# Issuing the keys' sign rows from ScalarE instead of the sync engine

## The chip, the cores and the metric

The kernel runs on one core of one Trainium2 chip. The metric is device microseconds of one execution, lower is better. Engines are named as in the profile: PE (TensorE), DVE (VectorE), ACT (ScalarE), POOL (GpSimd), SP (the sync engine, which here does nothing but issue transfers).

## The reference

Three layers run one after the other on 2 batches of 768 tokens, in float32.

```python
# 1: attention of 8 heads of 64, masked by a hash of 6 sign bits
q_bits = (einsum('bhsd,dk->bhsk', q, proj) > 0); k_bits = (einsum('bhsd,dk->bhsk', k, proj) > 0)
mask = bucket(q_bits)[:, :, :, None] == bucket(k_bits)[:, :, None, :]
scores = where(mask, scale * q @ k.T, -1e9); attn_out = softmax(scores) @ v
# 2: token mixing of low rank (U, V), then a feed-forward layer 512 -> 2048 -> 512 with a residual
u = x + (x.T @ U @ V).T;  x = u + relu(u @ w_ch1) @ w_ch2
# 3: four attention experts with a causal mask, two of them chosen per token by a gate
out += gate[e] * (softmax(causal(scale * q_e @ k_e.T)) @ v_e) @ wo[e]
```

Only the first layer is touched: a query sees a key only where all six sign bits agree.

## The kernel before

Every large product is made of float16 halves (a high part and a rest), so that it keeps float32's precision. The first layer goes through 8 pairs of heads (2 batches, 4 pairs each). For one pair the operands are AQ, AK (the high parts and rests), BQ, BK (64 rows of products' rests, and below them 32 rows of signs, rows 64 to 95, `SIGN`). `a1_head` makes the scores of 128 queries against 768 keys by a matmul of AQ and AK (L621) and one of BQ and BK over 96 rows (L626); the sign rows add a large number where the bits differ, which is the mask. DVE takes the row's extreme (L632), ACT the exponential (L543), ACT and POOL split the result into halves HL (L545, L551), a transposing transfer turns HL into PT (L643), and PE multiplies PT with V (L555 to L557). Some tiles are transposed on PE instead (L597).

The operands of the next pair are prepared while the present pair's heads run: `a1_prep` (L443 on) loads and splits q and k and moves rows into place with twelve transfers (L452 to L463), and six head tiles later `signs` (L466 on) multiplies the operands with the projection (L477), turns the result into sign rows in one DVE instruction (L482, tile SG), and moves those rows in four transfers of 32 rows x 768 float16: for each of the two heads one into BQ (L486) and one into BK (L487). This happens for pairs 1 to 7, so 28 transfers; pair 0 writes its signs in place. The same stage, up to about 300 us, loads and splits the weights of layer two (L277, L280) and begins its matmuls (L748, L770).

All transfers of the program are issued from SP's queue. The order of the instructions within every engine, SP among them, is laid down when the program is built: a planner takes instructions by a priority that follows the program text and by when its own timeline has them ready. An engine runs its list strictly in that order. Each transfer raises one of eight completion semaphores; the program uses the eight in turn, in the planned order of the transfers, and a transfer is issued only once the transfer that had the semaphore before it, the eighth before, has landed.

Of the kernel before, what the change touches and what calls it, by code (L numbers as in the profile page):

```python
# [22 lines left out]
def kernel(  # L23
# [17 lines left out]
    nc = tc.nc  # L41
# [86 lines left out]
    def halves(n):  # L128
        return [(c, min(512, n - c)) for c in range(0, n, 512)]
# [240 lines left out]
    def later(n, fn):  # L370
        pending.append([n, fn])
# [39 lines left out]
    SIGN = slice(D, D + 32)  # L411
# [3 lines left out]
    def a1_operands(b, p):  # L415
        n = f"{b}_{p}"
        AQ = sp.tile([P, 2, S], FH, tag="AQ", bufs=2, name=f"AQ_{n}")
        AK = sp.tile([P, 2, S], FH, tag="AK", bufs=2, name=f"AK_{n}")
        V = sp.tile([P, 2, 2 * NT, D], FH, tag="V", bufs=2, name=f"V_{n}")
        BQ, BK = BQK[p % 2]  # L420
        preps[b, p] = (AQ, AK, BQ, BK, V)
        return preps[b, p]
# [20 lines left out]
    def a1_prep(b, p, wait):  # L443
        qn, kn, vn = nats.pop((b, p))
        n = f"{b}_{p}"
        AQ, AK, BQ, BK, V = a1_operands(b, p)
        TQ = sp.tile([P, 2, S], FH, tag="TQ", name=f"TQ_{n}")
        HQ, LQ = TQ[:, 0], TQ[:, 1]
        nc.scalar.activation(HQ, qn, AF.Copy, scale=-0.125)
        nc.vector.scalar_tensor_tensor(LQ, HQ, 8.0, qn, op0=ALU.mult, op1=ALU.add)  # L450
        for j, o in enumerate(HALF):
            nc.sync.dma_start(AQ[HALF[0], j], HQ[o])  # L452
            nc.sync.dma_start(AQ[HALF[1], j], LQ[o])
            nc.sync.dma_start(BQ[HALF[0], j], HQ[o])
        TK = sp.tile([P, 3, S], FH, tag="TK", name=f"TK_{n}")
        HK, SK, LK = TK[:, 0], TK[:, 1], TK[:, 2]
        nc.scalar.activation(HK, kn, AF.Copy)
        SKE(SK, kn, HK)
        KLE.tensor_tensor(LK, kn, HK, op=ALU.subtract)
        for j, o in enumerate(HALF):  # L460
            nc.sync.dma_start(AK[HALF[0], j], HK[o])
            nc.sync.dma_start(AK[HALF[1], j], SK[o])
            nc.sync.dma_start(BK[HALF[0], j], LK[o])  # L463
        a1_values(b, p, vn, V)

        def signs():  # L466
            sg = psc.tile([P, 1024], F32, tag="sc", name=f"sg_{n}")
            for c0, cn in halves(S):
                cs = slice(c0, c0 + cn)

                for last, ops in enumerate((
                    [(PQ, AQ[:, j]) for j in range(2)] + [(PK, AK[:, j]) for j in range(2)],
                    [(PL, AQ[:, j]) for j in range(2)]
                    + [(PB, BK[HALF[0], j]) for j in range(2)],
                )):
                    for i, (w, x) in enumerate(ops):
                        nc.tensor.matmul(  # L477
                            sg[32 * i : 32 * (i + 1), cs], w, x[:, cs],
                            start=(last == 0), stop=(last == 1), skip_group_check=True,
                        )  # L480
            SG = sp.tile([P, S], FH, tag="KS", bufs=2, name=f"SG_{n}")
            nc.vector.tensor_scalar(  # L482
                SG, sg[:, 0:S], thr[:, 0:1], far, op0=ALU.is_lt, op1=ALU.mult
            )
            for j in range(2):
                nc.sync.dma_start(BQ[SIGN, j], SG[32 * j : 32 * (j + 1)])  # L486
                nc.sync.dma_start(BK[SIGN, j], SG[64 + 32 * j : 96 + 32 * j])  # L487

        later(wait, signs)

    def a1_values(b, p, vn, V):
        f32 = any(x[0] == "F" for x in A1_MODES[b][p])
        V32 = VF[p % 2] if f32 else vn
        nc.gpsimd.tensor_scalar(V32, vn, 16.0, 1.0, op0=ALU.mult, op1=ALU.mult)
        nc.scalar.activation(V[:, 0], V32, AF.Copy)
        nc.gpsimd.tensor_tensor(V[:, 1], V32, V[:, 0], op=ALU.subtract)
# [814 lines left out]
```

## Time and profile before

| | us |
|---|---|
| median of three runs | 607.75 |
| the three runs | 604.22, 607.75, 609.76 |
| the profiled execution | 604.46 |
| its span, first to last instruction | 602.7 |

The time is device time of one execution. The profile is of one execution; its span is counted from the first to the last instruction of the program, and 604.46 - 602.7 = 1.8 us lie around it. Instruction durations are read from this execution. "SPq" marks an issue on SP's queue: its duration is the time that the issuing takes, not the transfer's way to its destination; the time from issue to landing is shown apart.

### The profile page before, as it was taken

Reading aid. Unit: us, or ns where it says so; the run is one execution under the profiler, and the core shown is the slowest. Engines: PE = TensorE matmul, PEld = TensorE weight load, DVE = VectorE, ACT = ScalarE, POOL = GpSimd, SP = SyncE. Lnnn points to the kernel's source line nnn. Section 1 sums busy time; section 2 is a strip of 40 time slices with the busy share of each in tenths; the row PEclk is TensorE's granted clock in tenths of the full one; section 3 lists DMA queues with packets and bytes.
Section 4 is the critical chain, followed back from the end, with each engine's and each line's share of the span. In section 5 each row is a group of like instructions: output and inputs, shape, how many; then the busy total and the mean of one; then the engine's idle time right before and its main releaser. Section 6 shows DMA issues by size and latency. Waiting matters only on the chain.

```text
span 602.7 us, 14989 instructions
## 1 busy us (share of the span) xinstructions
PE 555.8 (92%) x5982; PEld 416.1 (69%) x5982; DVE 412.1 (68%) x948; ACT 351.9 (58%) x753; POOL 260.3 (43%) x239
## 2 busy tenths in 40 slices
PE   3789996899899999799999989999999998999995
PEld 1468864776555545447888866878877898999754
DVE  6976897759999999858768455553564335455584
ACT  6798787767564665645768534672465216144683
POOL 6644579745967698622246400250134002002350
PEclk9889999999899999999999999999999999999998
DMA  8789899989999999782479910153046002004655
GB/s 268 170 174 179 225 209 263 187 216 216 316 190 208 237 216 240 159 197 63 92 133 141 177 25 10 36 94 92 4 86 125 36 1 46 12 18 41 121 106 114
DMA packets 176566, 82.00 MB, mean 136 GB/s; under 512 B 160368, under 2 KB 167152, under 8 KB 176496
## 3 DMA queue, kind: packets, MB, share of 16 engines
q1 hardware_dynamic: 176496, 81.04, 62.2%
q8 instruction: 47, 0.77, 0.6%
q14 instruction: 23, 0.19, 0.1%
HBM read 29.30 MB, written 3.15 MB: 54 GB/s over the span
## 4 chain that ended last, share of the span: by engine, by line
PE 59%; DVE 16%; DMA 11%; issue 5%; ACT 5%; POOL 2%; SPq 1%; DVEq 0%; ACTq 0%; POOLq 0%
PE px L824 12%; PE ph L806 11%; DMA PT<-HL 6%; PE px L770 3%; PE po L606 3%; DVE P L632 2%; PE pk L875 2%; PE pq L875 2%; PE sc L621 2%; PE sc L626 2%; PE pv L903 2%; PE ph L748 2%; PE pz L1106 2%; PE s L974 2%; DMA wx<-in_moe_w_ch_dram 2%
## 5 line engine op out<-in xcount | busy, mean ns | idle before, releaser
L551 POOL TENSOR_TENSOR HL<-P,HL 128x768 f16<-128x768 f32 (+5 forms) x91 | 121.3, 1338 | 258.4 <-ACT HL L545 197.2
L543 ACT ACTIVATE P<-P,m 128x768 f32<-128x768 f32 (+5 forms) x110 | 89.4, 813 | 40.7 <-DVE P L632 26.2
L806 PE MATMUL ph<-U,W 128*128 128x256 f16 (+1 forms) x960 | 95.4, 251 | 0.5 <-DVE hT L808 0.5
L824 PE MATMUL px<-hT,W 128*128 128x256 f16 (+1 forms) x960 | 94.1, 251 | 0.0
L824 PEld LDWEIGHTS <-W 128*128 128x128 f16 x960 | 78.2, 98 | 8.4
L806 PEld LDWEIGHTS <-W 128*128 128x128 f16 x960 | 77.0, 98 | 8.7 <-issue 0.8
L632 DVE TENSOR_SCALAR_CACHE_REDUCE P<-sc 128x768 f32<-128x768 f32 x80 | 74.9, 947 | 11.0 <-PE sc L626 10.9
L545 ACT ACTIVATE HL<-P 128x768 f16<-128x768 f32 (+5 forms) x91 | 63.1, 696 | 9.7 <-DMA PT<-HL 8.5
L555 PEld LDWEIGHTS <-PT 128*128 128x128 f16 x522 | 47.6, 98 | 16.8 <-DMA PT<-HL 8.3
L621 PE MATMUL sc<-AK,AQ 128*128 128x512 f16 x192 | 49.0, 335 | 6.2 <-DVE P L632 2.7
L556 PEld LDWEIGHTS <-PT 128*128 128x128 f16 x522 | 47.4, 98 | 5.4 <-issue 1.9
L555 PE MATMUL po<-V,PT 128*128 128x64 f16 x378 | 43.5, 193 | 6.6 <-DMA PT<-HL 3.2
L626 PE MATMUL sc<-BK,BQ 96*128 96x512 f16 x192 | 49.6, 336 | 0.0
L557 PEld LDWEIGHTS <-PT 128*128 128x128 f16 x522 | 47.5, 98 | 1.7 <-issue 0.2
L770 PE MATMUL px<-hT,W 128*128 128x512 f16 x192 | 44.4, 379 | 0.8 <-DVE acc L754 0.4
L808 DVE SCALAR_TENSOR_TENSOR hT<-ph,hT 128x256 f16<-128x256 f32 (+1 forms) x80 | 28.8, 366 | 23.1 <-ACT hT L807 22.3
L557 PE MATMUL po<-V,PT 128*128 128x64 f16 x378 | 44.2, 193 | 0.0
L556 PE MATMUL po<-V,PT 128*128 128x64 f16 x378 | 44.2, 193 | 0.0
L807 ACT ACTIVATE hT<-ph 128x256 f16<-128x256 f32 (+1 forms) x80 | 26.4, 334 | 28.9 <-PE ph L806 28.0
L748 PE MATMUL ph<-U,W 128*128 128x512 f16 x156 | 36.3, 380 | 1.7 <-DVE hT L756 1.3
L982 DVE TENSOR_SCALAR_CACHE_REDUCE P<-s 128x128 f32<-128x128 f32 (+5 forms) x48 | 29.3, 620 | 9.1 <-PE s L979 8.0
L770 PEld LDWEIGHTS <-W 128*128 128x128 f16 x192 | 18.1, 98 | 20.6 <-DVE acc L754 0.8
(257 smaller groups left out, 1252.1 us busy)
## 6 DMA issues: line engine op xcount, KB each, us to landing
w<-in_moe_w_ch_dram SPq DMA_DIRECT2D x17, 512.0 KB, 5.1
wx<-in_moe_w_ch_dram SPq DMA_DIRECT2D x15, 512.0 KB, 5.6
vn<-in_v_dram SPq DMA_DIRECT2D x8, 384.0 KB, 4.5
out_dram<-o SPq DMA_DIRECT2D x12, 256.0 KB, 2.1
kn<-in_k_dram SPq DMA_DIRECT2D x7, 384.0 KB, 4.6
qn<-in_q_dram SPq DMA_DIRECT2D x7, 384.0 KB, 4.0
AK<-TK SPq DMA_DIRECT2D x28, 96.0 KB, 2.7
AQ<-TQ SPq DMA_DIRECT2D x28, 96.0 KB, 3.1
```

Source lines behind the costliest of these rows:

```text
L543: nc.scalar.activation(P32, P32, AF.Exp, bias=m, scale=-1.0, accum_out=ssum)
L545: nc.scalar.activation(HL[:, 0], P32, AF.Copy)
L551: eng.tensor_tensor(HL[:, 1], P32, HL[:, 0], op=ALU.subtract)
L555: nc.tensor.matmul(o, PT[:, t, :], vh(t), start=(t == 0), stop=False)
L556: nc.tensor.matmul(o, PT[:, t, :], vl(t), start=False, stop=False)
L557: nc.tensor.matmul(o, PT[:, nk + t, :], vh(t), start=False, stop=(t == nk - 1))
L621: nc.tensor.matmul(ps[:, c0 : c0 + cn], aq[:, P * t : P * (t + 1)], ak[:, c0 : c0 + cn], start=True, stop=False,)
L626: nc.tensor.matmul(ps[:, c0 : c0 + cn], bq[:, P * t : P * (t + 1)], bk[:, c0 : c0 + cn], start=False, stop=True,)
L632: nc.vector.tensor_scalar(P32, ps[:, 0:S], CLIP, None, op0=ALU.min, op1=ALU.min, accum_out=m)
L770: nc.tensor.matmul(po, w, u, start=(i == 0), stop=(i == len(ops) - 1))
L806: nc.tensor.matmul(ph, w, u, start=(i == 0), stop=(i == len(ops) - 1))
L824: nc.tensor.matmul(po, w, u, start=(i == 0), stop=(i == len(ops) - 1))
```

## The change

The two moves of sign rows into BK are issued from ScalarE's queue. The two into BQ, and all other transfers, stay on the sync engine. What is moved, where from and where to, is unchanged.

```diff
             for j in range(2):
                 nc.sync.dma_start(BQ[SIGN, j], SG[32 * j : 32 * (j + 1)])
-                nc.sync.dma_start(BK[SIGN, j], SG[64 + 32 * j : 96 + 32 * j])
+                nc.scalar.dma_start(BK[SIGN, j], SG[64 + 32 * j : 96 + 32 * j])
```

## Rows read from the trace of the kernel before

**Rows 1.** The page: busy time by engine; the chain that ended last.

```profile
PE 555.8 (92%) x5982; PEld 416.1 (69%) x5982; DVE 412.1 (68%) x948; ACT 351.9 (58%) x753; POOL 260.3 (43%) x239
...
PE 59%; DVE 16%; DMA 11%; issue 5%; ACT 5%; POOL 2%; SPq 1%; DVEq 0%; ACTq 0%; POOLq 0%
```

**Rows 2.** Windows: stretch, its length, busy us by engine, granted clock, DMA share, GB/s.

```profile
31.00:71.00 40.00, 37.88 (x374) 30.97 (x373) 30.18 (x59) 33.06 (x68) 20.75 (x15) 0.91 0.90 186
71.00:115.00 44.00, 36.73 (x440) 29.18 (x439) 37.26 (x72) 35.23 (x67) 33.15 (x26) 1.00 1.01 229
155.00:200.00 45.00, 42.54 (x366) 23.20 (x365) 42.67 (x76) 24.27 (x46) 32.22 (x29) 0.96 1.03 226
300.00:400.00 100.00, 95.96 (x1117) 76.83 (x1116) 61.57 (x160) 59.82 (x138) 31.74 (x29) 1.00 0.51 89
```

**Rows 3.** Timeline of SP at pair 2: start us, us, engine, line, what.

```profile
60.43 2.92 SPq L643 DMA_TRANSPOSE more_hT<-more_X  x1
63.45 1.02 SPq L486 DMA_DIRECT2D BQ<-SG  x1
...
65.78 0.59 SPq L487 DMA_DIRECT2D BK<-SG  x1
```

**Rows 4.** Line L487, the moved transfers: issue ns min/median/max; who waited for it; landing.

```profile
L487 SPq DMA_DIRECT2D BK<-SG x14: 517/588/1195, 41.2 to 294.9; - x14
...
  DVE wo L208: 0.7, 1
...
DMA to landing us min/median/max: 1.9/2.3/5.4
```

**Rows 5.** Line L643, the transposing transfers issued from SP: ns min/median/max.

```profile
L643 SPq DMA_TRANSPOSE PT<-HL x58: 1277/1483/3982, 35.7 to 344.9; - x58
```

**Rows 6.** Waits of PE from 31 to 300 us: us, times, longest.

```profile
PE po L555 <- DMA PT<-HL: 2.1, 1, 2.1
PE po L555 <- DMA PT<-more_X: 2.1, 2, 1.2
```

**Rows 7.** Timeline of DVE: sign rows of pair 1 and pair 3 made.

```profile
31.00 1.07 DVE L482 TENSOR_SCALAR SG<-sg,thr,far 128x768 f16<-128x768 f32 x1 [0.47 <-PE sg L477]
...
89.07 1.07 DVE L482 TENSOR_SCALAR SG<-sg,thr,far 128x768 f16<-128x768 f32 x1
```

**Rows 8.** Timeline of SP after the signs of pair 1.

```profile
32.08 3.48 SPq L236 DMA_DIRECT2D vs<-in_moe_V_dram  x7
...
38.24 0.59 SPq L486 DMA_DIRECT2D BQ<-SG  x1
...
41.16 0.79 SPq L487 DMA_DIRECT2D BK<-SG  x1
```

**Rows 9.** Line L626 at pair 1: the first matmul that reads the signs.

```profile
L626 PE MATMUL sc<-BK,BQ x1: 634/634/634, 43.8 to 43.8; 96*128 96x512 f16 x1
```

**Rows 10.** Timeline of ACT: first idle after signs, pairs 1, 2, 3, 6, 7.

```profile
39.51 0.94 ACT L543 ACTIVATE P<-P,m 128x768 f32<-128x768 f32 x1 [0.18 <-DVE P L632]
...
63.20 0.94 ACT L543 ACTIVATE more_X<-more_X,m 128x768 f32<-128x768 f32 x1 [0.41 <-DVE more_X L632]
...
96.26 0.94 ACT L543 ACTIVATE more_X<-more_X,m 128x768 f32<-128x768 f32 x1 [1.91 <-DVE more_X L632]
...
229.95 0.63 ACT L280 ACTIVATE W<-w 128x512 f16<-128x512 f32 x1 [2.70 <-DVE w L195]
...
292.59 0.94 ACT L543 ACTIVATE P<-P,m 128x768 f32<-128x768 f32 x1 [1.07 <-DVE P L632]
```

**Rows 11.** Timeline of SP: a load that holds the semaphore of pair 3's move.

```profile
88.43 0.86 SPq L403 DMA_DIRECT2D vn<-in_v_dram  x1
```

**Rows 12.** The page: transfers by line, KB each, us from issue to landing.

```profile
vn<-in_v_dram SPq DMA_DIRECT2D x8, 384.0 KB, 4.5
...
vs<-in_moe_V_dram SPq DMA_DIRECT2D x8, 96.0 KB, 2.6
```

## The prediction

> **What bounds the kernel now.** I began with the page's busy times and the chain that ended last [rows 1]: PE is busy for 92% of the span and holds 59% of the chain, ACT 5%, SP's queue 1%. Then the stretches [rows 2]. From 300 us on PE works 96 of 100 us at full clock and the DMA engines are half idle; the change doesn't reach there, as the moves end at 294.9 us [rows 4]. From 31 to 115 us PE works 37.88 + 36.73 = 74.6 of 84 us and ACT 33.06 + 35.23 = 68.3 (81%), so ACT has 15.7 us to spare there; from 155 to 200 us it is busy 24 of 45. The DMA engines are full in these stretches (share 0.90 to 1.03). Third, SP's own queue: around pair 2 it issues without a gap, a transpose for 2.92 us, then the sign rows from 63.45 to 66.37 [rows 3]. Last, the moved lines: nobody on PE waited for the landing of the keys' sign rows; one 0.7 us wait is all there is [rows 4].
>
> So three resources are near their limit in the first 300 us: PE, the DMA engines, and SP's time to issue. The change gives SP time back and takes it from ACT.
>
> **What SP gains.** Fourteen issues leave SP. The median is 588 ns [rows 4], so 14 x 0.588 = 8.2 us of SP time. What can that bring? Transposes queued behind the moves start earlier. PE's recorded waits for their landing come to 2.1 + 2.1 = 4.2 us in all of 31 to 300 us [rows 6]; that is the upper bound as long as SP isn't itself what paces the stage (then see the second rival), and the lower is nothing, because transfers released earlier meet full DMA engines. I take the middle, 2.1 us.
>
> **What an earlier landing of the signs gains.** Pair 1 is the tightest: the signs are ready at 31.00 + 1.07 = 32.07 [rows 7], SP issues loads first and moves the first key rows only at 41.16 [rows 8], and PE first reads them at 43.8 [rows 9]. Adding the median landing of 2.3 us [rows 4] gives 43.5, just in time. From ScalarE they could go out some 9 us sooner, but PE would have nothing to read sooner with: the first query rows stay on SP. Worth nothing.
>
> **What ACT pays to issue.** No row shows a transfer issued from ACT. Its cost lies between nothing (it is prepared while the instruction ahead still runs) and 1.195 us, the longest on SP [rows 4]; I take SP's median of 0.588, since the row is of the same transfer. That is 1.18 us a pair. The next idle time of ACT after the signs hides it: 0.18 us in pair 1 and 0.41 in pair 2, but 1.07 to 2.70 in pairs 3 to 7, of which three rows stand for five [rows 10]. What is left uncovered is 1.00 + 0.77 + 0.11 (pair 7) = 1.9 us. Queued behind an uncovered issue stand the exponentials (L543) and HL copies (L545), for which POOL's rests and then the transposes wait.
>
> One row speaks for a higher price: the issue that stands right behind a transpose took 1.02 us against 0.59 for one behind a plain move [rows 3], as if it had to wait for something that the transpose still held. The Trainium skill (Perfetto Trace Analysis, section DMA Instruction — HWDGE (DVE, Sync)) says that the block which generates descriptors is locked for one issue at a time and is shared by sequencers; the trace's 1.02 us agrees, though no run here has two issuers. By it ACT would queue behind SP's transposes, and the sum would be that of the first rival.
>
> **What ACT pays to wait.** If the moved transfers keep their turn among the eight semaphores, ACT can issue one only when the eighth transfer before it has landed; on SP that was no matter, as SP had issued those itself. Pair 1: its two key moves follow the fourth and the sixth of the seven vs loads, issued every 0.5 us from 32.08 [rows 8], so at about 33.6 and 34.6, landing 2.6 us later [rows 12]: 36.2 and 37.2. An ACT that arrives when the signs are ready (32.07) stands until 37.2, for 5.1 us. Pair 3: the second move follows a vn load issued at 88.43 [rows 11] that lands 4.5 us later [rows 12], at 92.9; the signs are ready at 90.14 [rows 7], so 2.8 us, of which the 1.91 - 1.18 = 0.7 us of idle time left hides some: 2.1. Two more pairs have a large load as the eighth before and are priced no higher, 2.1 each. Upper bound 5.1 + 3 x 2.1 = 11.4 us; lower bound nothing, if the planner puts the move into ACT's list where SP would have reached it. I take half, 5.7.
>
> **The sum.** ACT loses 1.9 + 5.7 = 7.6 us. The share that reaches the end lies between its share of the chain, 5%, and all; most of it falls into 31 to 115 us, where ACT is busy 81% and feeds everything behind it, so I take 0.6: 4.6 us. Less SP's 2.1: +2.5 us. Against the profiled execution's own 604.46 (span 602.7 and 1.8 around it) that gives 607.0. That execution lies 3.3 us under the median of the runs, 607.75, so the same change on the median gives 610.3; I say 610. Its own bounds: 607.75 - 4.2 = 603.5 (ACT's cost hidden, all waits for transposes gone) and 607.75 + 1.9 + 11.4 = 621.
>
> **Rival 1, slower: ACT queues behind SP's transposes.** The place is ACT's list, right after each pair's signs. If an issue from ACT must wait out a running transpose, of 1.48 us median [rows 5], it costs 0.59 + 1.48 = 2.07 us and 14 of them 29 us. Cover of some 0.6 us in pairs 1 and 2 and 1.5 in each of the other five takes off 8.1: 21 us lost, 0.6 of it passed on, less 2.1 for SP: +10.5, so 618. It decides (more than 1%, 6.1 us) from an issue price of (8.2 / 0.6 + 8.1) / 14 = 1.55 us. For it: SP's queue without gaps and the 1.02 us row [rows 3]. Against it: ACT's idle time, 15.7 us in the tightest stretch [rows 2].
>
> **Rival 2, faster: SP's issuing is what paces the first 200 us.** Then all 8.2 us come off: 607.75 - 8.2 = 599.5 (-1.4%). For it: the gapless rows of SP [rows 3], and transposes that hold it for 1.48 us each [rows 5]. Against it: full DMA engines [rows 2], SP's 1% of the chain [rows 1] and only 4.2 us of waits for transposes on PE [rows 6]. The Trainium skill (Perfetto Trace Analysis, section DMA Optimizations) says that where the issuing engine looks solid with slices, spreading transfers over engines may help; the trace agrees on the solid slices around pair 2 and by that rule the result would be this rival's.
>
> **Rival 3: another order.** The planner lays out all engines' lists from its own timeline. With two moves on another queue it may order the work of the first 300 us differently, for better or worse. No row prices it; I let it reach as far as rivals 1 and 2.
>
> **How the numbers follow.** About 1% is what a measurement of this kernel can tell from no change. Forecast 0.48, rival 1 0.27, rival 2 0.15, rival 3 0.10, half to each side. Faster by over 1% (under 601.7): 0.12 of rival 2, 0.04 of rival 3, 0.02 of the forecast, 0.18. Slower by over 1% (over 613.8): 0.25 of rival 1, 0.05 of rival 3, 0.08 of the forecast's upper end, 0.38. Within 1%: 0.44. The range from 600 to 621 leaves out about 0.1 at either end. The likeliest case's own range is 603.5 to 621.
>
> **What would show it.** Right: fourteen BK<-SG issues on ACT's queue of about 0.6 us; ACT's idle time after the signs of pairs 1 and 3 newly put down to a transfer, with 5 and 2 us at most; stretches after 300 us of unchanged length. Rival 1 would show in ACT issues of 1.5 us and more; rival 2 in a stage from 31 to 200 us that is shorter by about 8 us with PE's waits for transposes gone; rival 3 in other lines standing next to each other on PE and ACT. The prediction fails if ACT's issues cost nothing, or if the planner moves work in bulk.

## The result and the profile after

The changed kernel takes 611.25 us (median), the kernel before, run beside it, 606.51 us. The ratio is 1.0064, with an interval from 1.0037 to 1.009: slower by 0.4 to 0.9%, some 4 us. (It leaves out disturbed runs, so it lies a little below the quotient of the medians.) The profiled execution took 611.1 us, its span is 609.4 us (before 604.46 and 602.7).

The page after: busy time by engine, then the queue of the moved transfers (packets, MB, share of the DMA engines' time), then the chain that ended last.

```profile
PE 560.2 (92%) x5982; PEld 418.1 (69%) x5982; DVE 409.2 (67%) x948; ACT 352.2 (58%) x753; POOL 262.1 (43%) x239
...
q10 hardware_dynamic: 672, 0.69, 0.4%
...
PE 60%; DMA 12%; DVE 12%; ACT 7%; issue 4%; POOL 3%; SPq 1%; ACTq 0%; DVEq 0%; POOLq 0%
```

Against [rows 1] the number of instructions is the same on every engine, and so is what ACT, DVE and POOL spend on them within 3 us. PE is busy 4.4 us longer for the same 5982 matmuls, and that is where one has to look. The queue of the two moves, q10, stands with 0% in the chain.

Three stretches of [rows 2], after:

```profile
31.00:71.00 40.00, 35.72 (x377) 29.39 (x371) 30.47 (x59) 32.30 (x67) 20.87 (x15) 0.96 1.00 221
71.00:115.00 44.00, 37.08 (x364) 27.51 (x362) 38.63 (x76) 34.99 (x68) 35.06 (x29) 0.92 0.96 224
300.00:400.00 100.00, 95.84 (x1142) 77.12 (x1141) 62.46 (x155) 59.22 (x131) 31.58 (x28) 1.00 0.51 91
```

In 71 to 115 us PE starts 364 matmuls where it started 440, for the same busy time, and its granted clock is 0.92 instead of 1.00. From 300 us on nothing has changed.

The first layer has 16 heads with 12 matmuls of line L626 each, 192 in all; counted by these, its progress can be compared. Two windows from the start to the end of the last of them (head 15), before and then after:

```profile
0.00:340.00 340.00, 305.81 (x3016) 207.71 (x3017) 277.04 (x501) 231.61 (x430) 208.10 (x185) 0.98 0.87 195
```

```profile
0.00:345.90 345.90, 311.83 (x3017) 211.35 (x3018) 274.24 (x501) 232.46 (x430) 209.97 (x186) 0.98 0.87 192
```

So 5.9 us are lost by that point. What follows takes 262.7 us before (602.7 - 340.0) and 263.5 us after: the loss lies in the first layer. PE's recorded idle time there is the same, 34.2 and 34.1 us; its busy time is 6.0 us longer, for one matmul more, at the same mean clock of 0.98.

Cut once more, from the 48th of these matmuls to the 96th, which is four heads' work (called heads 4 to 7 below), before and after:

```profile
75.10:139.00 63.90, 55.14 (x641) 43.27 (x640) 49.29 (x93) 47.82 (x92) 43.06 (x31) 1.00 0.95 225
```

```profile
76.60:144.90 68.30, 59.88 (x631) 46.28 (x630) 53.03 (x102) 48.98 (x94) 49.55 (x38) 0.93 0.90 219
```

4.4 of the 5.9 us are lost in these four heads, by these two executions. PE is 4.7 us longer busy with 10 matmuls fewer, at a granted clock of 0.93. DVE and POOL have more to do in the same stretch, 9 and 7 instructions more; they belong to the conversion of layer two's weights, whose loads (L277) now stand earlier. By 100 us 11 of them are issued, 8 before. That brings up the lists: the planner made others. Counted in the two traces by line, operation and tiles, another instruction stands at 1754 of PE's 5982 places, 350 of DVE's 948, 307 of ACT's 753 and 99 of POOL's 239.

The moved line after (issue ns min/median/max; landing), to be read against [rows 4]:

```profile
L487 ACTq DMA_DIRECT2D BK<-SG x14: 514/581/1004, 32.6 to 299.8; - x14
...
DMA to landing us min/median/max: 2.5/3.9/6.5
```

The issue costs on ACT what it cost on SP. The landing takes 1.6 us longer, and nothing waits for it. ACT's timeline after the signs of pair 1, and then of pair 2:

```profile
32.30 0.84 ACT L545 ACTIVATE HL<-P 128x768 f16<-128x768 f32 x1
32.65 0.59 ACTq L487 DMA_DIRECT2D BK<-SG  x1
33.03 0.93 ACT L591 ACTIVATE more_X<-more_X,m 128x768 f32<-128x768 f32 x1
33.27 0.60 ACTq L487 DMA_DIRECT2D BK<-SG  x1
...
58.95 0.53 ACTq L487 DMA_DIRECT2D BK<-SG  x1
58.97 0.93 ACT L591 ACTIVATE more_X<-more_X,m 128x768 f32<-128x768 f32 x1
59.52 0.60 ACTq L487 DMA_DIRECT2D BK<-SG  x1
```

Here the issue keeps nothing from running. It runs while the instruction ahead of it is still running (32.30 to 33.14), and the next begins before the issue has ended. In pair 7 it does keep one waiting; ACT's timeline, and DVE's last instruction that the ACTIVATE needed:

```profile
299.28 1.17 ACTq L487 DMA_DIRECT2D BK<-SG  x2
300.50 0.39 ACT L807 ACTIVATE hT<-ph 128x256 f16<-128x256 f32 x1 [1.29 <-DVE hT L808]
...
299.73 0.38 DVE L808 SCALAR_TENSOR_TENSOR hT<-ph,hT 128x256 f16<-128x256 f32 x1
```

DVE is done at 300.11, and the ACTIVATE starts at 300.50, right behind the second issue: 0.4 us, the only such case among the fourteen issues. SP's timeline at the same time as the pair 2 issues:

```profile
58.81 2.34 SPq L643 DMA_TRANSPOSE more_hT<-more_X  x1
```

Both issues from ACT lie inside SP's issue of a transpose and take 0.53 and 0.60 us. Whether SP paid for them isn't settled: the two transposing issues up to 310 us that overlap one from ACT took 2.34 and 1.72 us, and the other 53 have a median of 1.49, but some of those took over 2.5.

So the change did what it says, ACT lost some 0.4 us by it, and the kernel is slower by ten times that. Two things changed at once, the queue and the order. The experiments take them apart.

### The profile page after: what moved, and what is told of

It reads as the page before. It is cut to its first block, busy times and chain, and to the rows that moved or that the text cites. A ratio compares the mean times of both kernels' runs of the same rounds, so it can differ in the third digit from the quotient of the medians.

```text
span 609.4 us, 14984 instructions
## 1 busy us (share of the span) xinstructions
PE 560.2 (92%) x5982; PEld 418.1 (69%) x5982; DVE 409.2 (67%) x948; ACT 352.2 (58%) x753; POOL 262.1 (43%) x239
## 4 chain that ended last, share of the span: by engine, by line
PE 60%; DMA 12%; DVE 12%; ACT 7%; issue 4%; POOL 3%; SPq 1%; ACTq 0%; DVEq 0%; POOLq 0%
PE px L824 12%; PE ph L806 11%; DMA PT<-HL 6%; PE px L770 5%; PE ph L748 3%; PE po L606 3%; PE pk L875 2%; PE pq L875 2%; PE pv L903 2%; PE sc L621 2%; PE sc L626 2%; PE pz L1106 2%; ACT P L543 2%; PE s L974 2%; POOL HL L551 2%
## 5 line engine op out<-in xcount | busy, mean ns | idle before, releaser
L806 PE MATMUL ph<-U,W 128*128 128x256 f16 (+1 forms) x960 | 97.9, 251 | 0.7 <-DVE hT L808 0.7
L632 DVE TENSOR_SCALAR_CACHE_REDUCE P<-sc 128x768 f32<-128x768 f32 x80 | 75.2, 948 | 13.6 <-PE sc L626 13.3
L824 PEld LDWEIGHTS <-W 128*128 128x128 f16 x960 | 78.1, 98 | 8.2
L621 PE MATMUL sc<-AK,AQ 128*128 128x512 f16 x192 | 50.3, 340 | 5.3 <-DVE P L632 2.8
L626 PE MATMUL sc<-BK,BQ 96*128 96x512 f16 x192 | 50.3, 338 | 0.0
L555 PE MATMUL po<-V,PT 128*128 128x64 f16 x378 | 44.8, 193 | 5.3 <-DMA PT<-HL 5.3
L557 PE MATMUL po<-V,PT 128*128 128x64 f16 x378 | 44.9, 193 | 0.0
L556 PE MATMUL po<-V,PT 128*128 128x64 f16 x378 | 44.6, 193 | 0.0
```

The costliest lines, as they stand in the source:

```text
L555: nc.tensor.matmul(o, PT[:, t, :], vh(t), start=(t == 0), stop=False)
L556: nc.tensor.matmul(o, PT[:, t, :], vl(t), start=False, stop=False)
L557: nc.tensor.matmul(o, PT[:, nk + t, :], vh(t), start=False, stop=(t == nk - 1))
L621: nc.tensor.matmul(ps[:, c0 : c0 + cn], aq[:, P * t : P * (t + 1)], ak[:, c0 : c0 + cn], start=True, stop=False,)
L626: nc.tensor.matmul(ps[:, c0 : c0 + cn], bq[:, P * t : P * (t + 1)], bk[:, c0 : c0 + cn], start=False, stop=True,)
L632: nc.vector.tensor_scalar(P32, ps[:, 0:S], CLIP, None, op0=ALU.min, op1=ALU.min, accum_out=m)
```

## The experiments

To keep an order, a program is planned twice: the second time each instruction is tied, in issue order only and without a wait, behind its neighbour in its engine's list of the first plan. So the lists of one kernel can be combined with the queue of the other; in the diffs, which are shortened to the lines that matter, the word after `planned(` is the queue of the key moves, and `order` the lists that are kept. The traces bear it out: in every run that keeps lists, ACT, DVE and POOL run the same instructions in the same order as in the kernel whose lists were kept, and so does PE where no spare matmuls are added.

### The order of before, the key moves on ACT

```diff
+    _, order = planned("sync", None)
+    nc, _ = planned("scalar", order)
```

> Every engine keeps the order that the planner made for the kernel before; only the 14 moves into BK are issued from ScalarE, at the places that they had in the planner's list. Theory Q (the queue itself costs: ScalarE's issues, its wait for the signs, two issuers at once): slower than before by about what the changed kernel is, 0.4 to 0.9%. Theory O (the queue is free, the new order of the other instructions costs): within 0.3% of before, or faster by up to 4.2 us (0.7%), as SP is relieved.

Measured: 604.51 us beside 606.03, ratio 0.9975 [0.9951, 0.9999]. The queue alone makes the kernel a little faster, 1.5 us, by an interval that ends just short of 1.

### The changed kernel's order, the key moves on SP

```diff
+    _, order = planned("scalar", None)
+    nc, _ = planned("sync", order)
```

> Every engine keeps the order that the planner made for the changed kernel; the 14 moves into BK are issued from the sync engine again, at the places that they had in the planner's list. Theory Q: as fast as before, within 0.3%. Theory O: slower than before by 0.4 to 0.9%, as the changed kernel is, or by more, if ScalarE's queue gave something back.

Measured: 612.65 us beside the same 606.03, ratio 1.0108 [1.0065, 1.0151]. The order alone costs 1.1%.

| ratio to before | key moves on SP | key moves on ACT |
|---|---|---|
| the order of before | 1 | 0.9975 [0.9951, 0.9999] |
| the order of after | 1.0108 [1.0065, 1.0151] | 1.0064 [1.0037, 1.009] |

The result is a larger loss by the order and a small gain by the queue. The gain is measured in the order of before; in that of after it doesn't stand clear of the noise (the changed kernel, measured once more below, came to 1.0124).

### The queries' rows on ACT instead, the planner free

```diff
-                nc.sync.dma_start(BQ[SIGN, j], SG[32 * j : 32 * (j + 1)])
+                nc.scalar.dma_start(BQ[SIGN, j], SG[32 * j : 32 * (j + 1)])
```

> The queries' rows (L486) go from ScalarE and the keys' stay on the sync engine; the planner is free. The transfers are of the same size and number. Theory Q: slower by 0.4 to 0.9%, as with the keys' rows. Theory O: another order and so another time; anything from -1 to +1.5%, and no reason to be near +0.6%.

Measured: 610.8 us, ratio 1.0104 [1.0061, 1.0148]. The planner made the same order as for the changed kernel: on PE, ACT, DVE and POOL not one instruction stands elsewhere than in the trace of after. So this is not a third order but the order of after measured again, with the other half of the moves on ACT, and it is slow again.

### All four moves on ACT, the order of before

```diff
-                nc.sync.dma_start(BQ[SIGN, j], SG[32 * j : 32 * (j + 1)])
+                nc.scalar.dma_start(BQ[SIGN, j], SG[32 * j : 32 * (j + 1)])
-                nc.sync.dma_start(BK[SIGN, j], SG[64 + 32 * j : 96 + 32 * j])
+                nc.scalar.dma_start(BK[SIGN, j], SG[64 + 32 * j : 96 + 32 * j])
```

> The order of the kernel before on every engine; all 28 moves of sign rows, the queries' too, are issued from ScalarE at their places in the planner's list. If what the queue gives is SP's time, twice the issues give up to twice as much: 0.992 to 0.997 of before. If it was the keys' earlier landing: 0.996 to 0.999, no more than with half of them. If ScalarE's waits for the signs begin to cost: over 1.000.

Measured: 602.67 us beside 605.51, ratio 0.9956 [0.9928, 0.9983]. Line L487 in this run, with L486 it makes 28 issues from ACT:

```profile
L486 ACTq DMA_DIRECT2D BQ<-SG x14: 514/522/606, 36.8 to 289.7; - x14
L487 ACTq DMA_DIRECT2D BK<-SG x14: 514/537/1578, 38.6 to 290.5; - x14
```

This is the fastest version found, and it beats both kernels. 28 issues taken from SP gain 2.8 us, 14 gained 1.5.

### What SP's time is worth: spare moves

Here SP gets more to do, with the lists of before. First, behind each key move two spare moves into rows 96 to 127 of BK, which nothing reads; the second must wait until the first has landed.

```diff
                 nc.sync.dma_start(BK[SIGN, j], SG[64 + 32 * j : 96 + 32 * j])
+                for x in range(2):
+                    nc.sync.dma_start(BK[96:128, j], SG[32 * (x + 1) : 32 * (x + 2)])
```

> The order of the kernel before; behind each of the 14 key moves SP issues two spare moves of 32 sign rows into rows of BK that nothing reads, 28 issues or 16.5 us of SP time more. If SP's time paces the first 300 us, the price of an issue that e1 suggests (1.5 us of 14 issues, 0.11 us each) gives +3 us, 1.003 to 1.009 of before. If SP has slack: within 0.2% of before.

Measured: 644.85 us, ratio 1.0654 [1.0618, 1.0689]. SP issued the 28 for 15 us and stood 29 us for the landings; the span is 39.2 us longer. The wait makes this a price of SP standing, not of issuing, so it was made again with one spare move into BQ and one into BK, which wait for nothing:

```diff
+                for x in (BQ, BK):
+                    nc.sync.dma_start(x[96:128, j], SG[64 + 32 * j : 96 + 32 * j])
```

> The order of the kernel before; behind each key move SP issues two spare moves of 32 sign rows into rows 96 to 127 of BQ and of BK, which nothing reads; unlike in the first run with spare moves, neither waits for the other to land. 28 issues, 16.5 us of SP time. If each us of SP time costs what SP's time cost there (39 us for some 46): 14 us, 1.02 to 1.025. If it costs what the issues taken away gave (0.1 us each): 3 us, 1.003 to 1.007. If the first run's loss was the waits alone: within 0.3% of before.

Measured: 620.66 us beside 605.6, ratio 1.025 [1.0213, 1.0287]: 15 us for 28 issues of 0.59 us, 16.4 us. (The spare moves also take time of the DMA engines; by q10's 0.4% of the span for 14 such moves that is 2.4 us for 14, about 5 us for 28, spread over 300 us.) Heads 4 to 7 in this run:

```profile
76.60:149.60 73.00, 60.68 (x640) 47.33 (x639) 51.66 (x96) 47.67 (x93) 43.53 (x32) 0.91 0.94 216
```

Against the 63.9 us of before PE is busy 5.5 us longer here for one matmul less, at a clock of 0.91. More work for SP costs much more (0.9 us per us) than less work gives (2.8 us of 16.4, or 0.2). So SP's queue is not what bounds the kernel as it stands. How much of the 15 us is SP's time isn't shown: the spare moves also take their turns among the eight semaphores, and the clock fell with them.

### Does the loss hang on the weight loads in SP's list?

In the order of after the 12th weight load stands ahead of two transposes, and SP stands for it. SP's timeline after:

```profile
96.63 0.43 SPq L277 DMA_DIRECT2D w<-in_moe_w_ch_dram  x1
101.27 0.33 SPq L277 DMA_DIRECT2D wx<-in_moe_w_ch_dram  x1
101.69 4.71 SPq L643 DMA_TRANSPOSE PT<-more_X  x2
```

From 97.06 to 101.27 SP issues nothing, 4.2 us, nearly the loss of the four heads. That was the theory: one load, issued early, holds up SP and the transposes behind it. Four runs were made on it. With the planner free, the loads held behind the transposes that they follow in the plan of before (key moves on ACT):

```diff
+        if name in TRANSPOSES:
+            before = name
+        elif name in LOADS:
+            if before is not None:
+                tc.add_manual_dep(here[name], before, kind, reason="place of a load")
```

> The changed kernel, but on SP every weight load (L277) stands behind the transposing transfer that it follows in the plan of the kernel before; all else is left to the planner. Theory L (the new order is slow because it brings three weight loads ahead of pair 3's transposes, where SP stands 4.2 us for a stage buffer): the loss is gone, 0.994 to 1.002 of before. Rival S (any other order than the one before is slower, whichever place the loads have): still slower, 1.003 to 1.012.

Measured: 613.45 us, ratio 1.0125 [1.008, 1.0171]. Heads 4 to 7:

```profile
76.60:140.70 64.10, 56.91 (x642) 44.56 (x639) 47.27 (x89) 47.31 (x91) 40.74 (x29) 0.97 0.91 201
```

The four heads have their 64 us again, POOL's and DVE's extra work is out of them, and the kernel is not faster for it: heads 8 to 15 take 205.7 us, where after took 201.0. (Runs with the lists of after show up to 205.5 there, so it isn't shown that this order is to blame.) The reverse, all moves on SP and the transposes tied behind the loads that are ahead of them in the plan of after:

```diff
+            behind = next((x for x in order[n:] if x in TRANSPOSES), None)
+            if behind is not None:
+                tc.add_manual_dep(here[behind], name, kind, reason="place of a load")
```

> All moves on the sync engine as before, but on SP the transposing transfers stand behind those weight loads that are ahead of them in the changed kernel's plan; all else is left to the planner. Theory L: slower, 1.006 to 1.013 of before, with SP standing some 4 us at about 97 us. Rival S: slower too if the order of the other engines moves much (so this run counts against L only if it is within 0.3% of before).

Measured: 617.99 us, ratio 1.017 [1.0125, 1.0214]. Slower than before, and no faster than after; the planner made yet another order, so this run doesn't separate the loads from the rest. Then the single suspect, all other lists kept as after has them: the 12th load put behind the two transposes.

```diff
+    for n, load in enumerate(loads[11:12]):
+        behind = sorted(place[x] for x in set(TRANSPOSES) if place[x] > place[loads[11]])
+        place[load] = behind[1] + (n + 1) / 1e3
```

> The changed kernel with its own order on every engine; only the 12th weight load, for whose stage buffer SP stood 4.21 us at 97 us with a transpose ready behind it, is issued behind the two transposing transfers that followed it. Theory L (that stand is the loss, or most of it): the six transposes there go out 3 to 5 us sooner and the time falls to 0.998 to 1.003 of before. Rival S (the loss is spread over the order): 1.004 to 1.009, as the changed kernel is.

Measured: 612.81 us, ratio 1.0106 [1.0066, 1.0146]; the four heads took 68.7 us. SP's timeline:

```profile
95.45 0.43 SPq L277 DMA_DIRECT2D w<-in_moe_w_ch_dram  x1
98.26 5.21 SPq L643 DMA_TRANSPOSE PT<-more_X  x2
103.56 0.53 SPq L277 DMA_DIRECT2D wx<-in_moe_w_ch_dram  x1
```

The stand fell from 4.2 to 2.4 us (95.88 to 98.26), the transposes went out 2.3 us earlier, counted from the load ahead of them, and nothing came of it. The theory falls. Loads 9 to 12 all moved in that way (`loads[8:12]`):

> The same with the 9th to the 12th weight loads, all four behind those two transposes. Theory L: as the run with one load or up to 0.2% better, 0.997 to 1.003; if the loads are then late for their conversion on DVE, a little worse than that run. Rival S: 1.004 to 1.009.

Measured: 613.51 us, ratio 1.0118 [1.008, 1.0157]. The same. The changed kernel itself stood beside these two runs on the same chip:

> The changed kernel once more, beside the other runs of this call on the same chip: 1.004 to 1.009 of before, as measured before. Both theories expect the same; it is the base that the two runs with moved loads are held against.

Measured: 613.83 us beside 605.6, ratio 1.0124 [1.0076, 1.0171]. The two intervals of after have only 1.0076 to 1.009 in common; taken together they put its loss between 0.4 and 1.7%. The runs with moved loads are no better than it.

### What the windows have in common

The first layer in three parts, each run's windows ending with the 48th, 96th and 192nd matmul of L626 (us; granted clock). Each row is one execution; the two of after differ by 4.7 us in all, mostly in heads 0 to 3:

| run | lists | heads 0 to 3 | heads 4 to 7 | clock there | heads 8 to 15 |
|---|---|---|---|---|---|
| before | before | 75.1 | 63.9 | 1.00 | 201.0 |
| key moves on ACT | before | 75.7 | 65.7 | 0.97 | 199.1 |
| all moves on ACT | before | 71.1 | 63.0 | 1.00 | 201.8 |
| after | after | 76.6 | 68.3 | 0.93 | 201.0 |
| after, once more | after | 80.1 | 69.1 | 0.93 | 201.4 |
| key moves on SP | after | 78.1 | 68.1 | 0.92 | 204.7 |
| 12th load moved | after, SP's changed | 75.0 | 68.7 | 0.93 | 205.5 |
| loads 9 to 12 moved | after, SP's changed | 75.1 | 71.2 | 0.88 | 204.1 |
| queries on ACT | after | 77.1 | 68.1 | 0.92 | 202.6 |
| loads held | own | 76.6 | 64.1 | 0.97 | 205.7 |

With the lists of after, heads 4 to 7 take 68 us or more at a clock of 0.93 or less, whatever the queue. They aren't the only ones that do: with the lists of before and spare moves on SP it was 73.0 us at 0.91. Windows of 3 us after:

```profile
93.00:96.00 3.00, 1.40 (x20) 1.41 (x21) 3.00 (x7) 2.97 (x8) 3.00 (x3) 0.65 1.13 301
96.00:99.00 3.00, 3.00 (x15) 2.60 (x15) 0.07 (x1) 0.80 (x2) 3.00 (x2) 0.50 1.06 313
...
117.00:120.00 3.00, 2.96 (x31) 2.96 (x32) 2.97 (x5) 1.08 (x2) 2.92 (x3) 0.63 0.55 127
```

and before, where PE is also half idle from 93 us on:

```profile
93.00:96.00 3.00, 1.72 (x16) 1.16 (x15) 1.33 (x2) 1.35 (x4) 2.92 (x3) 1.00 1.16 290
96.00:99.00 3.00, 1.85 (x30) 1.41 (x30) 3.00 (x8) 2.67 (x7) 3.00 (x3) 1.00 1.10 214
```

The granted clock falls to its lower level (0.50, 1.2 GHz) twice in these heads after and not at all before. PE's timeline after shows what stood ahead of each fall, and DVE's, in the second fence, what stood ahead of that:

```profile
94.60 0.24 PE L555 MATMUL po<-V,more_hT 128*128 128x64 f16 x1 [1.79 <-DMA more_hT<-HL]
...
98.14 0.85 PE L621 MATMUL sc<-AK,AQ 128*128 128x512 f16 x2
...
117.04 2.18 PE L606 MATMUL po<-more_hT,more_hT 128*128 128x64 f32 x12 [2.37 <-DVE xn L652]
```

```profile
92.93 0.70 DVE L189 TENSOR_SCALAR w_x<-wx 128x512 uint32<-128x512 uint32 x1 [1.22 <-DMA wx<-in_moe_w_ch_dram]
...
116.44 0.55 DVE L652 TENSOR_TENSOR xn<-po,r 128x384 f32<-128x384 f32 x1
```

PE waits 1.79 us for a transpose, and 2.37 us for xn; behind either the clock is at 1.2 GHz, and a pair of score matmuls takes 0.85 us instead of 0.49. Three more runs with the lists of after show the same two waits with the same releasers, and a fall to 0.50 or 0.6 behind each: key moves on SP (1.33 and 2.36 us), after once more (2.06 and 2.36), 12th load moved (1.56 and 2.36). Length alone doesn't decide it, since before has waits of 1.57 and 1.69 us at 96.28 and 101.05 us with the clock at 1.00.

Two things speak against making the clock the whole cause. Before has a fall of its own, from 39 to 48 us, which after doesn't have (0.91 and 0.96 in the window from 31 to 71 us), and over the whole first layer the mean is 0.98 in both kernels, though after takes 5.9 us longer. And heads 0 to 3 take 1.5 us longer after, at the better clock of 0.98 instead of 0.93.

### PE kept busy over the two waits

The last experiment is to take the clock's fall away and leave the order: 18 spare matmuls of identity by identity, 8 ahead of the first wait and 10 ahead of the second, into PSUM columns that nothing reads then. All else of the lists is that of after.

```diff
+                more = [nc.tensor.matmul(po8[:, NT:, :], ident, ident, start=True, stop=True).ins.name for _ in range(8)]
...
+                for _ in range(10):
+                    x = nc.tensor.matmul(held[0][:, 0:P], ident, ident, start=True, stop=True)
```

> The changed kernel with every list in its own order, and 18 spare matmuls in TensorE's list (identity by identity, 128x128 float32, about 0.21 us each at full clock): eight directly ahead of the values' matmul that waited 1.79 us for a transpose at 94.6 us, ten directly ahead of the one that waited 2.37 us for xn at 117.0 us. They write columns of PSUM that nothing reads at that time, so nothing that is computed changes. Behind these two stands, and nowhere else in heads 3 to 7, the granted clock of the changed kernel fell to 1.2 GHz: windows of 3 us show 0.65, 0.50, 0.71 from 93 to 102 us and 0.63, 0.80 from 117 to 123 us, some 10 us at the lower level, worth about 5 us of TensorE's work; before shows 1.00 throughout. Theory C, the clock's fall is what costs heads 3 to 7 their 4.4 us (68.3 against 63.9): with TensorE kept busy over the stands the clock stays at 0.97 or above there, the stretch shortens to 64 to 66 us, and the whole run comes to 0.998 to 1.004 of before. Theory W, what the new order makes the other engines wait for (VectorE stands 1.22 us for a weight load at 92.9 us, and the transposes and xn come late) sets the pace, and the slower matmuls were hidden behind it: the stretch stays at 67.5 to 70 us whatever the clock shows, and the run at 1.006 to 1.013.

Measured: 607.64 us beside 603.86, ratio 1.0074 [1.0041, 1.0107]; span 607.4 us. Windows of this run, heads 4 to 7 and three of 3 us (the lines of this kernel are counted on: L625 is L621 of before, L643 is L632):

```profile
77.20:143.20 66.00, 60.47 (x667) 47.50 (x666) 53.75 (x101) 48.72 (x94) 49.65 (x38) 0.97 0.98 224
93.00:96.00 3.00, 2.98 (x38) 2.54 (x36) 2.12 (x4) 2.97 (x7) 3.00 (x3) 1.00 1.11 268
96.00:99.00 3.00, 3.00 (x35) 2.49 (x32) 1.72 (x5) 2.01 (x5) 3.00 (x3) 1.00 1.07 285
105.00:108.00 3.00, 2.57 (x11) 1.68 (x10) 3.00 (x6) 1.10 (x3) 2.84 (x3) 0.50 1.07 205
```

Where PE was kept busy, at 93 to 99 us, the clock stayed at 1.00. The four heads take 66.0 us at 0.97, 2.3 and 3.1 less than in the two runs of after. But PE then ran into a longer wait for DVE further on, 1.85 us until 104.29, and the clock fell there instead:

```profile
104.29 0.49 PE L625 MATMUL sc<-AK,AQ 128*128 128x512 f16 x2 [1.85 <-DVE P L643]
105.75 0.80 PE L625 MATMUL sc<-AK,AQ 128*128 128x512 f16 x2 [0.43 <-DVE U L209]
```

Neither theory holds alone. Theory C had these heads right and the whole kernel wrong, theory W the reverse. In heads 4 to 7 about half of the loss came back, and the rest stands beside the fall that was left: with the lists of before and the key moves on ACT they take 65.7 us at the same 0.97. So there the time goes with the clock more than with the order. For the whole first layer the clock isn't the cause: this run has a granted clock of 0.99 over its 344.7 us, and before has 0.98 over its 340.0.

```profile
0.00:344.70 344.70, 312.90 (x3053) 212.56 (x3054) 279.27 (x501) 232.07 (x430) 209.81 (x186) 0.99 0.88 192
```

For the whole kernel the ratio can't be told from that of after (1.0064 and 1.0124), so a gain of the whole is not shown.

## Why the prediction came out as it did

The forecast was 610 us and slightly slower, and 611.25 us was measured. The number is right by luck; the sum that led to it is not. In its order:

**What bounds the kernel.** Right as far as it goes: nothing changed from 300 us on, and the loss lies among the first heads. What it left out is that this balance holds for one order only.

**What SP gains.** 2.1 us were taken, from nothing to 4.2. With the order held, 14 issues less gave 1.5 us. The size was right. Its reason, shorter waits of PE for transposes [rows 6], isn't confirmed: with the key moves on ACT and before's order they are 2.9 + 1.7 = 4.6 us from 31 to 300 us, no less than the 4.2 before. The trace of one execution doesn't show where so small a gain lies.

**An earlier landing of the signs is worth nothing.** Right. The first key rows of pair 1 went out at 32.65 us instead of 41.16 [rows 8], but its first query rows, still on SP, at 39.93, and PE's first matmul that reads both started at 45.06 (before 43.8 [rows 9]).

**What ACT pays to issue.** This step failed. Its median of 0.588 us was right (0.581 measured), its place was not: the issue was set against ACT's idle time [rows 10], as if ACT couldn't compute meanwhile. The timelines of pairs 1 and 2 show the issue running beside the ACTIVATE ahead and the one behind, with no gap, and in pair 7 0.4 us are lost. Near the lower end, nothing, was the value; 1.9 us were charged.

**What ACT pays to wait.** This step failed too, and it was the largest term, 5.7 us. No moved issue stood for a transfer. The waits were reckoned from the order of before, in which a large load stands eight transfers ahead [rows 8, 11]; in the order of after the first issue of every pair went out 0.03 to 0.04 us after its sign rows were made, and the second 0.55 to 0.62 us behind the first. In the run with before's order the first move stands in ACT's list at 40.43 us, about where SP had it; there, too, no idle time of ACT beside the moves is put down to a transfer. That was the lower bound named in the text, and the value to take.

**The sum.** Its ACT terms, 4.6 us, come to some 0.4; in their place stands a term that the sum didn't have, the new order, +1.1% or 6.6 us. That both have one sign is chance.

**Rival 1** (ACT queues behind SP's transposes) is refuted by the rows at 58.81 and 58.95. By the lock for one issue at a time of which the Trainium skill (Perfetto Trace Analysis, section DMA Instruction — HWDGE (DVE, Sync)) speaks, it would have come. In pair 2 the trace doesn't bear that out for ACT, with 0.53 and 0.60 us inside an SP issue of 2.34 us; whether SP waited instead, it doesn't tell. **Rival 2** (SP paces the stage) was right in its sign and wrong in its size: 1.5 us of 8.2. The rule named there (the Trainium skill, Perfetto Trace Analysis, section DMA Optimizations), that spreading transfers may help where an issuing engine looks solid, holds with the order kept: -0.25% for 14 moves, -0.44% for 28. **Rival 3** (another order) is the cause. It was named, and given 0.10 and no price, because no row shows it. Its mark, other lines standing next to each other on PE, was there at 1754 of PE's 5982 places, and the sentence that the prediction fails "if ACT's issues cost nothing, or if the planner moves work in bulk" came true in both halves, the first but for 0.4 us.

**What stays open.** Which decision of the planner costs what isn't settled. Shown is that the lists as a whole cost 1.1%, that moving SP's early loads alone doesn't bring it back, and that keeping the clock up at two places gives back about half of the loss in heads 4 to 7, though not a measurable part of the whole; what the first layer loses at a clock no lower than before's is not explained. That the weight conversion brought forward, DVE and POOL doing 9 and 7 instructions more in these heads, makes DVE late and so lengthens PE's waits is argued from the rows (DVE stands 1.22 us for a weight load at 92.93 us with score tiles waiting), and the run with the loads held, where that work is out of these heads and they take 64.1 us, agrees; the conversion moved on all engines with all else kept wasn't tried.

## What to carry to other kernels

Where a planner lays out the order, an edit of one line is two edits: hold every engine's list fixed to measure the edit itself, and price the new order as a term of its own, of either sign. A small transfer issued from an engine that computes can be nearly free, so look whether its queue runs beside its work before charging it against idle time; once the order is held, moving issues off a full queue gains a little (here all 28 on ACT: 602.67 us, 0.44% less). And read a stretch's granted clock beside PE's busy time: the same matmuls, busier, can be a wait just ahead of them.

## What the runs showed of the hardware that was not expected

- An issue on ACT's queue, 0.51 to 0.61 us in 13 of 14 cases, overlaps ACTIVATEs on both sides and SP's issue of a transpose. One took 1.00 us, at 175.25, begun while SP still issued a transpose; the same issue took 1.11 us in after once more and 1.03 with the queries on ACT, each beside a transpose. With all moves on ACT one took 1.58 us, with no issue on SP beside it; what lengthens them isn't settled. In the changed kernel SP's issues of the query rows have a median of 703 ns (before 582), and the key rows land in 3.9 us (before 2.3 [rows 4]); with before's order kept and the key moves on ACT the medians are 582 ns and 3.3 us. What made the difference wasn't tried.
- Giving SP 16.4 us more to issue cost 15 us; taking 8.2 or 16.4 us away gave 1.5 or 2.8.
- Waits of PE of 1.33 to 2.37 us were followed by some microseconds at 1.2 GHz in the order of after, and waits of 1.57 and 1.69 us in heads 4 to 7 of before were not; what decides it is not settled here.
